# Attention followed by a SiLU layer on one core: an earlier load of the second couple's q, the first q transposed in two halves, and two re-ordered groups of instructions

## Chip, cores, metric

The kernel runs on one core of a Trainium2 chip. The metric is the device time of one execution in microseconds (us). A core has a matrix engine (TensorE, PE in the profile; PEld is its loading of weights), VectorE (DVE), ScalarE (ACT), GpSimd (POOL) and SyncE (SP), which here only issues DMAs. Each engine works off its own queue in order and waits for the others through semaphores.

## What is computed

```python
# q, k, v: (8 batches, 12 heads, 448 rows, 64), g_q, g_k: (64,)
q_n = q / sqrt(mean(q * q, -1) + 1e-6) * g_q         # k_n likewise, with g_k
scores = q_n @ k_n.T / sqrt(64)                      # per batch and head
attn = exp(scores - max) / (sum(exp(scores - max)) + 1e-9)
x = (attn @ v), heads side by side                   # (3584, 768)
h = x @ w_in                                         # w_in: (768, 2048)
out = (h * sigmoid(h)) @ w_out                       # w_out: (2048, 768)
```

## The kernel before

The heads are taken in pairs, and two pairs (four heads of one batch) are a *couple*: 24 couples, three per batch; `c` is a couple's number. One group of six couples (`GROUP` = 6) is two batches. While a group goes through attention, the first product (with `w_in`) of the group before it is computed beside it; its matrix products use seven half-size products in place of eight (class `Seven`), and so need sums and differences on VectorE and GpSimd. After all attention the rest of the first product and the whole second one follow. The gains are folded into k's transposes, and the softmax needs no maximum when the gains are small enough: a branch (line 369) tests that once, and the branch taken here is `bounded`.

**Before the branch** (lines 296 to 359) a fixed order is written out: loads of the first q, k and v on SyncE's queue, the two gains on ScalarE's, a few matmuls on the identity that only keep TensorE busy (`keep_busy`, line 342), and the root mean squares of q and k of couple 0. `Norm` does these: squares on ScalarE and their sums on VectorE (`squares`, lines 395 and 396), scaling by 1/64 on VectorE (line 420), the power -1/2 on GpSimd (line 424), the product with the rows (`scale`, line 439; on VectorE for couple 0, on GpSimd for later ones). Each of q's steps is done in two halves, one for each pair of heads.

**After it**, SyncE issues the loads of q of couples 1 and 2 and of weights; k and q of couple 0 are transposed on TensorE (lines 561 and 546) and copied out of PSUM by ScalarE (lines 563 and 547). Then `visit(c)` and `between(c)` alternate. A visit computes scores (line 579, into tiles `sc` of two banks, two of them in turn), their exponentials on ScalarE (line 584), and the products with v (`weigh`, line 611, into the banks `av0` and `av1`); the last two products of a couple are made in the next visit. Spread over the visits lie the four pieces of `normalise` for the next couple (`beside`): squares of the two halves of q, then of the two halves of k. From couple 1 to 5 the second of them stands, in the order of instructions, after the copies of the previous couple's products (line 1250), after its division (line 669) and after the reciprocals of the sums of exponentials (line 654), which are then spread over the partitions by six small DMAs (lines 660 and 662). A q piece ends, for couples below six, with the load of q two couples further on into the same buffer.

`between(c)` transposes the next couple's q and k, sums the exponentials (line 645, in a bank `mm`) and deals out two portions of other work with `fill`: matmuls of the first product are drawn one at a time from a generator until a number of columns is reached, and other instructions are dealt among them: the rounding of weights on ScalarE, VectorE and GpSimd (lines 90, 91, 113 to 120, 124), reciprocals, sums. In couples 3 to 5 the generator is `make_ahead`: for each of two blocks it makes two products of three matmuls (`two`, with `product`, line 745), the first copied out by ScalarE (line 752), the second added to it by VectorE (lines 753 and 704), and saves the result. `product` hands control back after every matmul, the last one included, so that what `fill` deals at that point comes ahead of the copy or the addition.

The order of instructions is the order of these calls; the scheduler is off (`manual_schedule`).

Of the kernel before, what the change touches and what calls it, by code (L numbers as in the profile page):

```python
# [27 lines left out]
BANK = 512  # L28
# [152 lines left out]
def kernel(  # L181
# [47 lines left out]
        left = rows[:, z.KEYS * P : z.S].rearrange("(i h) p d -> i p h d", i=2)  # L229
        return main, left  # L230

    def load_q(c, t, by_head):


        b, cp = divmod(c, z.NPAIR // 2)
        rows = q[b, ts(cp, 4)]
        if by_head:
            dst = t[0:R].rearrange("p (n j d) -> p n (j d)", n=4, j=J)
            nc.sync.dma_start(dst, rows.rearrange("n (p j) d -> p n (j d)", j=J))
            return  # L240
        for i in range(2):
            dst = t[0:R, ts(i, nq // 2)].rearrange("p (j h d) -> p j h d", j=J, h=2)
            nc.sync.dma_start(dst, rows[ts(i, 2)].rearrange("h (p j) d -> p j h d", j=J))
# [29 lines left out]
    def load_pair(state, n):  # L273
# [3 lines left out]
        for i, (name, source, bufs) in enumerate((("q", q, 2), ("k", k, 3), ("v", v, 2))):  # L277
# [15 lines left out]
    most = const.tile([1, 1], F32, name="most")  # L293
    norm = Norm(nc, z, rms, minus_half)

    first_q = room.rest[:, ds(7 * nq, nq)]
    first_squares = [spare[:, 0 : 2 * J * D], room.rest[:, ds(6 * nq, nq // 2)]]
    g1, both = (
        room.rest[0:1, ds(room.rest.shape[1] - (i + 1) * 2 * D, 2 * D)].rearrange(
            "p (two d) -> p two d", two=2  # L300
        )
        for i in range(2)
# [1 line left out]
    with tc.manual_schedule(), tc.tile_pool(  # L304
        name="ps_first", bufs=1, space=bass.MemoryType.PSUM
    ) as ps_first:
        load_q(0, first_q, True)
        load_k(0)
        for i, g in enumerate((g_q, g_k)):
            nc.scalar.dma_start(g1[:, i, :], g.rearrange("(one d) -> one d", one=1))  # L310
        load_k(1)
        load_v(0)
        load_v_rest(0)
        room.w_in.load()
        load_v_rest(1)
        nc.gpsimd.memset(minus_half, -0.5)
        make_identity(nc, ident)
        nc.scalar.activation(first, minus_half, AF.Square)


        nc.gpsimd.memset(ones[:, 0], 1.0)
        for i in range(2):
            for half in range(2):
                rows = ds(half * z.LEFT, z.LEFT)
                nc.gpsimd.memset(ones[rows, 1 + i], 1.0 if i == half else 0.0)

        wide = [g1[:, i : i + 1, :].to_broadcast([1, 2, D]) for i in range(2)]
        nc.vector.tensor_tensor(out=both, in0=wide[0], in1=wide[1], op=ALU.mult)
        nc.vector.tensor_reduce(
            out=most, in_=both[:, 0, :], axis=AX.X, op=ALU.max, apply_absolute_value=True  # L330
        )
        nc.vector.tensor_scalar(
            out=small, in0=most, scalar1=float(SCORE_MAX / D**0.5), scalar2=None, op0=ALU.is_le
        )


        idle = ps_first.tile([P, P], F32, name="idle")
        column = ps_first.tile([P, BANK], F32, name="column")[:, 0:1]

        def keep_busy(n):  # L340
            for _ in range(n):
                nc.tensor.matmul(idle, ident, ident, start=True, stop=True)

        keep_busy(4)
        nc.tensor.transpose(column, both.rearrange("p two d -> p (two d)"), ident[0:1, 0:1])
        nc.vector.tensor_scalar_mul(out=gains, in0=column, scalar1=float(D) ** -0.5)
        keep_busy(8)

        for i in range(2):
            norm.squares_q(0, first_q, first_squares[i], i)  # L350
            norm.root(0, "q", i)
        for i in range(2):
            norm.squares_k(0, place["k0"], first_squares[i], i)
            norm.root(0, "k", i)
            norm.scale(0, first_q, place["q0"], i, nc.vector)

    def arm():

        r = copy.copy(room)
        r.w_in = copy.copy(room.w_in)  # L360
        state = [dict() for _ in pairs]
        return dict(
            tc=tc, nc=nc, z=z, pairs=pairs, room=r, ring=ring, w_out=w_out, ident=ident,
            minus_half=minus_half, gains=gains, out=out,
            own=dict(NC=NC, loads=loads, place=place, norm=norm, spare=spare, ones=ones, first=first),
            plain=(state, lambda n: load_pair(state, n)),
        )

# [88 lines left out]
def bounded(  # L457
# [51 lines left out]
    for i, words in enumerate(late):  # L509
# [3 lines left out]
        low = words.rearrange("p (n two) -> p n two", two=2)[:, :, 0]  # L513
        pieces[m] = pieces[m][:2] + ((None, words), low)

    def q_of(c):
        return rows_q[c % 2 if c < GROUP else 0]

    def load_q(c):

        if 0 < c < GROUP:
            loads["q"](c, raw_q[c % 2], True)
        elif GROUP <= c < NC:
            loads["q"](c, q_of(c), False)

# [14 lines left out]
    def transpose_q(c):  # L540

        t = ps.tile([P, 2, BANK], F32, name="sc", bufs=2)
        for i in range(2):
            for j in range(J):
                rows = q_of(c)[0:R, ts(i * J + j, 2 * D)]
                nc.tensor.transpose(t[:, i, ts(j, R)], rows, ident[0:R, 0:R])  # L546
        nc.scalar.copy(qT, t[:, :, 0:S])
        if c == GROUP - 2:
            load_q(GROUP)
        elif c >= GROUP:  # L550
            load_q(c + 1)
# [121 lines left out]
    def normalise(c):  # L673


        if c >= NC:
            return []

        def piece(name, i):
            t = scratch[i if c < GROUP + 2 else 0]  # L680
            source = raw_q[c % 2] if c < GROUP else q_of(c)
            if name == "q":
                norm.squares_q(c, source, t, i)
            else:
                norm.squares_k(c, place[f"k{c % 2}"], t, i)
            if name == "q" and c < GROUP:
                norm.root(c, name, i)
                norm.scale(c, source, q_of(c), i, nc.gpsimd)
                if i == 1 and c + 2 < GROUP:
                    load_q(c + 2)  # L690
            elif i == 1:
                norm.root(c, name)
                if name == "q":
                    for m in range(2):
                        norm.scale(c, source, q_of(c), m, nc.gpsimd)

        return [lambda a=a: piece(*a) for a in (("q", 0), ("q", 1), ("k", 0), ("k", 1))]
# [34 lines left out]
    class Seven:  # L732

        def __init__(self, left, right, steps, n, done):
            self.left, self.right, self.steps, self.n, self.done = left, right, list(steps), n, done
            self.u2, self.u3 = (parts[:, ds(i * S, n)] for i in range(2))

            self.p1, self.p5 = done[1, 2], done[2, 1]  # L740

        def product(self, name):
            t, ends = bank(self.n), (self.steps[0], self.steps[-1])
            for s in self.steps:
                nc.tensor.matmul(  # L745
                    t, self.left(name, s), self.right(name, s), start=s == ends[0], stop=s == ends[1]
                )
                yield self.n
            return t

        def two(self):
            nc.scalar.copy(self.p1, (yield from self.product("1")))
            plus((yield from self.product("2")), self.p1, self.done[1, 1])

        def five(self):
            p1, u2, u3, p5, done = self.p1, self.u2, self.u3, self.p5, self.done
# [22 lines left out]
    def make_ahead(group):  # L779
        for m in range(AHEAD):  # L780
            row = staged()
            yield from part_in(group, m, [row, row]).two()
            nc.sync.dma_start(ahead[m], row)

    def fetch_ahead(group, m):
# [25 lines left out]
    def sum_x(group, c):  # L811
        right_sums(*quarters(group, c), *sums_of_x(c))

    def part_in(group, m, rows):

        chunk = 2 * m // room.CHUNK
        assert room.w_in.rounded >= (chunk + 1) * z.NW
# [19 lines left out]
            return lefts[name](c)  # L837

        done = {(i + 1, j + 1): rows[i][:, ts(j, S)] for i in range(2) for j in range(2)}
        return Seven(left, right, range(HW), S, done)  # L840

    def halves_in(group, blocks, beside=lambda m: iter(()), begun={}, fetched=()):

# [389 lines left out]
    def visit(c):  # L1233
# [7 lines left out]
            weigh(c - 1, LEFT - 1, 0)  # L1241
        if c < NC:
            scores(c, 0, 1)
        if not 0 < c < GROUP:
            run_all(beside[1:2])
        if c > 0:
            weigh(c - 1, LEFT - 1, 1)
            if c - 1 < EARLY:
                for i in range(2):
                    nc.vector.tensor_copy(x_of(c - 1, i), sums[i])  # L1250
                if inverting:
                    if c > 1:
                        divide(c - 2, None)
                    run_all(inverting)
                    inverting.clear()
            else:
                divide(c - 1, sums)
                if c < NC and c % GROUP == 0:
                    for i in range(0 if c == GROUP else 1, HW):
                        sum_x(last_two(c), i)  # L1260
                weights_in_visit(c)
            if c < GROUP:
                run_all(beside[1:2])
            if c + 1 < NC:
                loads["vrest"](c + 1)
        if c == NC:
# [18 lines left out]
    def run_all(work):  # L1285
        for piece in work:
            piece()
# [44 lines left out]
                pass  # L1332

    begun, inverting = {}, []
    for c in (1, 2):
        load_q(c)
    for _ in range(2):
        room.w_in.load()
    transpose_k(0)
# [230 lines left out]
```

## Time and profile before

| what | value |
|---|---|
| median of 3 runs | 1363.62 us (1363.23 to 1364.3) |
| the profiled execution's own time | 1364.13 us |
| its span, first to last instruction | 1362.3 us |
| granted TensorE clock, mean | 0.995 |
| PE busy | 1325.9 us, 97% |
| DVE / ACT / POOL busy | 918.5 / 517.6 / 342.7 us |
| first scores (line 579) begin | 12.35 us |
| q of couple 1 transposed (line 546), first matmul | 28.86 us |
| q of couples 2, 3, 4, 5, 6, first matmul | 46.33, 63.09, 80.59, 100.79, 125.77 us |
| PE busy from 200 to 800 us | 591.8 of 600 us |
| loads of a whole q, 448 KB, issue to landing | 4.1 us median |
| loads of k's main part, 192 KB | 3.0 us median |

In a line of the timeline the first number is the start in us, the second the duration; then come the engine, the source line, the operation, what it writes and reads with shapes, and how many instructions are merged. In brackets stands how long the engine had been idle before, and whose work ended that. One fp32 matmul appears as two records. In a table of stretches each engine's busy time is followed by its number of instructions; after the five engines come the clock granted to TensorE (1.00 is full), the busy share of the DMA engines, and GB/s.

### The profile page before, as it was taken

The numbers are of one execution on the slowest core, as the hardware profiler recorded it, in microseconds if no ns is written. First come the engines' busy times: TensorE is split into PE (matmuls) and PEld (weight loads), VectorE is DVE, ScalarE is ACT, GpSimd is POOL, SyncE is SP. The second block draws the span as 40 slices with busy tenths as digits, with TensorE's granted clock in tenths as the row PEclk, the third lists the DMA queues.
The fourth block names the chain that finished last, engine by engine and source line by source line (L and its number), as shares of the span: only waits on it lengthen the run. The fifth ranks groups of instructions, "written<-read, shape, count | busy, mean of one in ns | idle before, by whom it ended". The sixth has DMA issues, their size and how long they took to land.

```text
span 1362.3 us, 19801 instructions
## 1 busy us (share of the span) xinstructions
PE 1325.9 (97%) x7353; PEld 838.3 (62%) x7353; DVE 918.5 (67%) x1592; ACT 517.6 (38%) x884; POOL 342.7 (25%) x241
## 2 busy tenths in 40 slices
PE   7998999999999999999999999999999999999997
PEld 3333444444444444444444455556999999999997
DVE  3887867785643544644543677679878787878785
ACT  5875565565455544555554244420000000000000
POOL 4664434342332233323320134420000000000001
PEclk8999999999999999999999999999999999999999
DMA  6664445333222322322221248531413232323321
GB/s 175 183 162 108 109 135 153 92 92 90 78 76 79 93 78 78 106 78 73 71 85 44 99 134 259 175 108 43 128 61 110 74 97 74 103 82 95 108 63 38
DMA packets 175405, 139.41 MB, mean 102 GB/s; under 512 B 104036, under 2 KB 159268, under 8 KB 175300
## 3 DMA queue, kind: packets, MB, share of 16 engines
q1 hardware_dynamic: 174624, 137.08, 34.3%
q8 instruction: 60, 0.98, 0.3%
q0 software_dynamic: 352, 0.79, 0.2%
q14 instruction: 45, 0.37, 0.1%
q10 hardware_dynamic: 324, 0.20, 0.1%
HBM read 88.47 MB, written 41.29 MB: 95 GB/s over the span
## 4 chain that ended last, share of the span: by engine, by line
PE 89%; DVE 5%; issue 3%; ACT 2%; SPq 1%; DMA 0%; POOL 0%; ACTq 0%; DVEq 0%; POOLq 0%
PE mm L745 29%; PE alone L1047 22%; PE av L611 8%; PE sc L579 8%; PE mm L1047 7%; PE alone L745 7%; PE alone L1084 2%; PE sc L546 1%; PE sc L561 1%; PE sc L645 1%; PE mm L645 1%; PE mm L1084 1%; DVE work L654 1%; ACT work L584 1%; DVE work L625 1%
## 5 line engine op out<-in xcount | busy, mean ns | idle before, releaser
L745 PE MATMUL mm<-x,W 128*128 128x448 f32 x636 | 255.5, 546 | 5.2 <-DVE stage L704 2.8
L584 ACT ACTIVATE work<-sc,rms 128x448 f32<-128x448 f32 x324 | 184.3, 632 | 88.5 <-PE sc L579 76.6
L424 POOL TENSOR_TENSOR rms<-rms,minus_half 128x14 f32<-128x14 f32 (+4 forms) x55 | 138.6, 2521 | 252.3 <-DVE rms L420 200.9
L745 PEld LDWEIGHTS mm<-x,W 128*128 128x128 f32 x636 | 118.3, 191 | 127.8 <-issue 107.3
L745 PE MATMUL mm<-sums_x,W 128*128 128x448 f32 x456 | 183.0, 542 | 0.8 <-DVE parts L704 0.8
L579 PE MATMUL sc<-work 64*64 64x448 f32 x1344 | 164.9, 548 | 6.7 <-ACT work L584 4.8
L625 DVE TENSOR_TENSOR work<-work 128x896 f32<-128x896 f32 (+1 forms) x114 | 125.0, 1130 | 59.0 <-ACT work L584 57.6
L611 PE MATMUL av<-work,rows 64*64 64x448 f32 x1296 | 153.9, 549 | 7.7 <-issue 2.4
L745 PEld LDWEIGHTS mm<-sums_x,W 128*128 128x128 f32 x456 | 85.3, 190 | 86.5 <-issue 81.1
L451 POOL DMA_DIRECT2D out_dram<-x x4 | 2.2, 565 | 442.7 <-DVE x L704 442.7
L611 PEld LDWEIGHTS av<-work,rows 64*64 64x64 f32 x1296 | 51.9, 133 | 96.4 <-issue 86.3
L579 PEld LDWEIGHTS sc<-work 64*64 64x64 f32 x1344 | 52.0, 134 | 89.6 <-issue 35.3
L396 DVE TENSOR_REDUCE rms<-squares 112x8 f32<-112x512 f32 (+1 forms) x80 | 52.4, 656 | 73.8 <-ACT squares L395 73.0
L1047 PE MATMUL alone<-W,rows 128*128 128x192 f32 x488 | 92.0, 326 | 0.0
L760 POOL TENSOR_TENSOR parts<-parts,stage 128x448 f32<-128x448 f32 x31 | 42.0, 1356 | 163.7 <-DVE parts L704 163.5
L1047 PEld LDWEIGHTS alone<-W,rows 128*128 128x128 f32 x488 | 81.4, 190 | 0.0
L1047 PE MATMUL alone<-W,work 128*128 128x192 f32 x382 | 72.2, 326 | 0.0
L878 ACT ACTIVATE stage<-stage 128x896 f32<-128x896 f32 x63 | 57.3, 945 | 26.1 <-DVE stage L704 25.4
L1047 PEld LDWEIGHTS alone<-W,work 128*128 128x128 f32 x382 | 63.8, 190 | 0.0
L654 DVE RECIPROCAL work<-sc 128x224 f32<-128x224 f32 x36 | 55.7, 1548 | 11.1 <-PE sc L645 11.1
L1057 ACT COPY squares<-alone 128x192 f32<-128x192 f32 x34 | 10.8, 318 | 136.9 <-PE alone L1047 78.4
L395 ACT ACTIVATE squares<-rows 128x512 f32<-128x512 f32 (+1 forms) x74 | 44.7, 605 | 47.1 <-DVE rms L396 46.3
(242 smaller groups left out, 2117.4 us busy)
## 6 DMA issues: line engine op xcount, KB each, us to landing
hidden<-stage SPq DMA_DIRECT2D x63, 448.0 KB, 2.8
work<-hidden SPq DMA_DIRECT2D x21, 1024.0 KB, 5.5
rows<-in_moe_w_out_dram SPq DMA_DIRECT2D x32, 384.0 KB, 3.2
W<-in_moe_w_in_dram SPq DMA_DIRECT2D x22, 512.0 KB, 5.1
rows<-in_k_dram SPq DMA_DIRECT2D x48, 192.0 KB, 3.0
work<-work SPq DMA_DIRECT2D x144, 56.0 KB, 1.9
rows<-in_q_dram SPq DMA_DIRECT2D x36, 224.0 KB, 3.5
x<-hidden SPq DMA_DIRECT2D x7, 1024.0 KB, 5.9
```

The lines of the kernel that those rows point to most:

```text
L395: nc.scalar.activation(t, rows, AF.Square)
L396: nc.vector.tensor_reduce(out=out, in_=t.rearrange("p (n d) -> p n d", n=n), axis=AX.X, op=ALU.add)
L424: nc.gpsimd.tensor_tensor(out=t, in0=t, in1=half, op=ALU.pow)
L579: nc.tensor.matmul(two[ds(half * D, D), h, 0:S], keys[rows, ts(half, D)], qT[rows, pair, :], start=True, stop=True,)
L584: nc.scalar.activation(eleft[:, h] if j == LEFT else weights(c, j)[:, i, h], two[:, h, 0:S], AF.Exp, scale=norm.column(c, i, h, j),)
L611: nc.tensor.matmul(sums[i][ds(h * D, D), :], v, w, start=(j == 0 and step == 1), stop=(j == LEFT - 1 and step == 1),)
L625: nc.vector.tensor_tensor(out=total, in0=total, in1=more, op=ALU.add)
L654: nc.vector.reciprocal(out=r[0][:, rows], in_=t[:, rows])
L745: nc.tensor.matmul(t, self.left(name, s), self.right(name, s), start=s == ends[0], stop=s == ends[1])
L760: nc.gpsimd.tensor_tensor(out=u2, in0=u2, in1=p5, op=ALU.add)
L878: nc.scalar.activation(t, t, AF.Silu)
L1047: nc.tensor.matmul(t, x[:, i], y, start=i == ORDER[0], stop=i == ORDER[-1])
```

## The change

- The first q is loaded in two halves, one per pair of heads.
- The load of q of couple 1 goes ahead of the branch, behind the first k, into a place of its own (`second_q`, the last 1024 columns of `room.rest`); the gains' scratch moves to make room. The load of v of couple 0 follows it, ahead of k of couple 1. After the branch only q of couple 2 is loaded. As couple 1's q has its own place, the load of couple 3's q no longer waits for couple 1's scaling.
- Of the twelve `keep_busy` matmuls the last four are left out.
- Couple 0's q: the transposes of the first pair go to a bank of `sc`, those of the second to `av1`; ScalarE copies the first (448 columns), VectorE the second.
- In visits 1 to 5 the second q piece (sum over the second half's squares, power, scaling, load of a later q) goes directly behind the copies of line 1250, ahead of division and reciprocals; in visit 6 it goes behind the division.
- In `make_ahead` control is handed back after the copy or addition, not between it and the last matmul.

In the compiled order TensorE differs only in the four matmuls left out and in the bank; VectorE has one copy more; on ScalarE and VectorE the copies and additions of `two` stand before the rounding that they followed; on SyncE the load of a later q stands ahead of the six spread DMAs of the same visit in visits 1 and 2 (visit 3 has none).

```diff
-    def load_q(c, t, by_head):
+    def load_q(c, t, by_head, steps=1):
...
         if by_head:
-            dst = t[0:R].rearrange("p (n j d) -> p n (j d)", n=4, j=J)
-            nc.sync.dma_start(dst, rows.rearrange("n (p j) d -> p n (j d)", j=J))
+            for i in range(steps):
+                n = 4 // steps
+                dst = t[0:R, ts(i, nq // steps)].rearrange("p (n j d) -> p n (j d)", n=n, j=J)
+                nc.sync.dma_start(dst, rows[ts(i, n)].rearrange("n (p j) d -> p n (j d)", j=J))
             return
...
-    first_q = room.rest[:, ds(7 * nq, nq)]
+    first_q, second_q = (room.rest[:, ds(i * nq, nq)] for i in (7, 8))
...
-        load_q(0, first_q, True)
+        load_q(0, first_q, True, 2)
         load_k(0)
+        load_q(1, second_q, True)
+        load_v(0)
         for i, g in enumerate((g_q, g_k)):
             nc.scalar.dma_start(g1[:, i, :], g.rearrange("(one d) -> one d", one=1))
         load_k(1)
-        load_v(0)
         load_v_rest(0)
...
-        keep_busy(8)
+        keep_busy(4)
...
+    def raw_of(c):
+        return own["second_q"] if c == 1 else raw_q[c % 2]
...
     def transpose_q(c):
         t = ps.tile([P, 2, BANK], F32, name="sc", bufs=2)
+        both = [t[:, i] for i in range(2)]
+        if c == 0:
+            both[1] = ps.tile([P, BANK], F32, name="av1")
         for i in range(2):
             for j in range(J):
                 rows = q_of(c)[0:R, ts(i * J + j, 2 * D)]
-                nc.tensor.transpose(t[:, i, ts(j, R)], rows, ident[0:R, 0:R])
-        nc.scalar.copy(qT, t[:, :, 0:S])
+                nc.tensor.transpose(both[i][:, ts(j, R)], rows, ident[0:R, 0:R])
+            if c == 0:
+                (nc.scalar.copy, nc.vector.tensor_copy)[i](qT[:, i], both[i][:, 0:S])
+        if c > 0:
+            nc.scalar.copy(qT, t[:, :, 0:S])
...
     class Seven:
...
                 nc.tensor.matmul(
                     t, self.left(name, s), self.right(name, s), start=s == ends[0], stop=s == ends[1]
                 )
-                yield self.n
+                if not (self.prompt and s == ends[1]):
+                    yield self.n
             return t
         def two(self):
             nc.scalar.copy(self.p1, (yield from self.product("1")))
+            if self.prompt:
+                yield self.n
             plus((yield from self.product("2")), self.p1, self.done[1, 1])
+            if self.prompt:
+                yield self.n
...
     def visit(c):
...
-        if not 0 < c < GROUP:
+        if c == 0:
             run_all(beside[1:2])
         if c > 0:
             weigh(c - 1, LEFT - 1, 1)
             if c - 1 < EARLY:
                 for i in range(2):
                     nc.vector.tensor_copy(x_of(c - 1, i), sums[i])
+                run_all(beside[1:2])
                 if inverting:
...
             else:
                 divide(c - 1, sums)
+                run_all(beside[1:2])
...
-            if c < GROUP:
-                run_all(beside[1:2])
...
-    for c in (1, 2):
-        load_q(c)
+    load_q(2)
```

`make_ahead` calls `part_in(group, m, [row, row], True)`, which hands `prompt=True` to `Seven`.

More of the change, by code (lines that the diff above doesn't have):

```diff
@@ L294 @@
     norm = Norm(nc, z, rms, minus_half)
-    first_q = room.rest[:, ds(7 * nq, nq)]
+    first_q, second_q = (room.rest[:, ds(i * nq, nq)] for i in (7, 8))
     first_squares = [spare[:, 0 : 2 * J * D], room.rest[:, ds(6 * nq, nq // 2)]]
     g1, both = (
-        room.rest[0:1, ds(room.rest.shape[1] - (i + 1) * 2 * D, 2 * D)].rearrange(
+        room.rest[0:1, ds(6 * nq + nq // 2 + i * 2 * D, 2 * D)].rearrange(
             "p (two d) -> p two d", two=2
@@ L364, in arm @@
             minus_half=minus_half, gains=gains, out=out,
-            own=dict(NC=NC, loads=loads, place=place, norm=norm, spare=spare, ones=ones, first=first),
+            own=dict(
+                NC=NC, loads=loads, place=place, norm=norm, spare=spare, ones=ones, first=first,
+                second_q=second_q,
+            ),
             plain=(state, lambda n: load_pair(state, n)),
@@ L521, in load_q @@
         if 0 < c < GROUP:
-            loads["q"](c, raw_q[c % 2], True)
+            loads["q"](c, raw_of(c), True)
         elif GROUP <= c < NC:
@@ L680, in piece @@
             t = scratch[i if c < GROUP + 2 else 0]
-            source = raw_q[c % 2] if c < GROUP else q_of(c)
+            source = raw_of(c) if c < GROUP else q_of(c)
             if name == "q":
@@ L732, in bounded, with __init__ @@
     class Seven:
-        def __init__(self, left, right, steps, n, done):
+        def __init__(self, left, right, steps, n, done, prompt=False):
             self.left, self.right, self.steps, self.n, self.done = left, right, list(steps), n, done
+            self.prompt = prompt
             self.u2, self.u3 = (parts[:, ds(i * S, n)] for i in range(2))
@@ L781, in make_ahead @@
             row = staged()
-            yield from part_in(group, m, [row, row]).two()
+            yield from part_in(group, m, [row, row], True).two()
             nc.sync.dma_start(ahead[m], row)
@@ L812, in sum_x, with part_in @@
         right_sums(*quarters(group, c), *sums_of_x(c))
-    def part_in(group, m, rows):
+    def part_in(group, m, rows, prompt=False):
         chunk = 2 * m // room.CHUNK
@@ L839, in part_in @@
         done = {(i + 1, j + 1): rows[i][:, ts(j, S)] for i in range(2) for j in range(2)}
-        return Seven(left, right, range(HW), S, done)
+        return Seven(left, right, range(HW), S, done, prompt)
     def halves_in(group, blocks, beside=lambda m: iter(()), begun={}, fetched=()):
```

## The prediction

> **What bounds the kernel.** I read the page first, then busy time in stretches cut at the transposes of each couple's q (line 546), then TensorE's timeline for the first 165 us, and for each gap the timeline of the engine named in the brackets.
>
> ```profile
> PE 1325.9 (97%) x7353; PEld 838.3 (62%) x7353; DVE 918.5 (67%) x1592; ACT 517.6 (38%) x884; POOL 342.7 (25%) x241
> ```
>
> TensorE (PE) is busy 97% of 1362.3 us; what is left is mostly at the start. Stretches (us; then busy time and instructions of PE, PEld, DVE, ACT, POOL; granted clock; DMA share; GB/s):
>
> ```profile
> 0.00:12.35 12.35, 7.44 (x41) 6.72 (x41) 5.12 (x14) 5.70 (x8) 6.86 (x16) 1.00 0.78 187
> 12.35:28.86 16.51, 12.33 (x89) 3.60 (x89) 4.54 (x9) 8.81 (x16) 8.02 (x6) 0.79 0.68 191
> 28.86:46.33 17.47, 16.48 (x155) 6.64 (x151) 12.91 (x20) 14.90 (x26) 7.74 (x7) 1.00 0.56 173
> 100.79:125.77 24.98, 21.78 (x165) 8.59 (x162) 17.42 (x24) 14.30 (x25) 10.57 (x6) 0.93 0.37 99
> ```
>
> Couple 0 (second row) loses most: PE idles 4.2 of 16.5 us, and its clock is reduced. From 200 us on PE is 98.5% busy or more until the last stretch, and every stage follows the one before in the same queues, so a microsecond won early should stay won. The gaps, by PE's timeline (start, duration, what; idle before it and its releaser):
>
> ```profile
> 12.35 1.73 PE L579 MATMUL sc<-work 64*64 64x448 f32 x16 [1.00 <-ACT work L547]
> 18.85 1.77 PE L579 MATMUL sc<-work 64*64 64x448 f32 x8 [3.20 <-ACT work L584]
> 47.32 0.60 PE L546 MATMUL sc<-ident,rows 112*128 112x112 f32 x4 [0.39 <-POOL rows L439]
> 64.75 0.60 PE L546 MATMUL sc<-ident,x 112*128 112x112 f32 x4 [1.05 <-POOL x L439]
> 82.22 0.60 PE L546 MATMUL sc<-ident,rows 112*128 112x112 f32 x4 [1.03 <-POOL rows L439]
> 110.66 3.36 PE L745 MATMUL mm<-x,W 128*128 128x448 f32 x4 [2.76 <-DVE stage L704]
> 132.41 2.52 PE L745 MATMUL mm<-x,W 128*128 128x448 f32 x6 [0.99 <-ACT stage L752]
> 141.74 1.12 PE L611 MATMUL av<-work,rows 64*64 64x448 f32 x6 [1.02 <-DVE x L669]
> ```
>
> The 3.20 us name ScalarE (ACT), but ACT itself waited: the squares of q of couple 1 stand ahead of the exponentials in its queue, and their load was issued only at 12.95, behind the branch.
>
> ```profile
> 17.12 0.63 ACT L395 ACTIVATE squares<-x 112x512 f32<-112x512 f32 x1 [2.50 <-DMA x<-in_q_dram]
> 17.65 1.14 ACT L584 ACTIVATE work<-sc,rms 128x448 f32<-128x448 f32 x2
> ```
>
> VectorE (DVE) explains the next ones: two reciprocals (2.96 us) stand ahead of the sums of q's second half, and 1.5 us of weight rounding ahead of the addition that frees a bank.
>
> ```profile
> 40.41 2.96 DVE L654 RECIPROCAL work<-mm 128x224 f32<-128x224 f32 x2
> 43.28 0.62 DVE L396 TENSOR_REDUCE rms<-x 112x8 f32<-112x512 f32 x1
> ...
> 108.52 0.36 DVE L113 TENSOR_SCALAR W<-W 128x512 f32<-128x512 f32 x1
> 108.92 0.43 DVE L116 TENSOR_SCALAR W<-W 128x512 int32<-128x512 int32 x1
> 109.38 0.69 DVE L120 SCALAR_TENSOR_TENSOR W<-W 128x512 int32<-128x512 int32 x1
> 109.99 0.62 DVE L704 TENSOR_TENSOR stage<-mm,stage 128x448 f32<-128x448 f32 x1
> ```
>
> [...] eight matmul records of line 579 take 0.98 us at 14.67 and 1.77 after the 3.2 us gap; the clock by the microsecond is 0.50 from 18.3 to 25.1 and again from 110.7 to 114.0. At the start the clock column reads 1.00, but the warming matmuls of line 342 last 421 ns each until 8.0 us and about 300 after; there I trust the durations. [...] Here the pair of line 625 takes 2.10 us at 27.45 and 2.94 at 45.28, beside POOL's scaling at 45.91.
>
> **Start.** Loading q in two halves wins nothing by itself: the first sum (line 396, 5.64) stands in DVE's queue behind the gains (line 346, until 5.60), which wait for g_k at 4.81. So POOL's powers and both scalings (8.39, 10.00) stay, and the second pair's transposes run at 10.75 to 11.35. Then PE waited for one ACT copy of both halves (0.91 us) until 12.35. Now ACT copies half 0 while PE waits for half 1, and DVE copies half 1 (as line 1250: 0.61); the first scores need only half 0 and start at 11.35: 1.0 won. DVE's copy comes behind its own branch (SP's takes 1.2 us, 11.74 to 12.95), hence at about 11.9 to 12.5; it delays only the second scores, needed by ACT at 14.0. The four warming matmuls left out (1.7 us at low clock) are covered by k's seven transposes, which move up to about 7.1, if k has landed. SP issues one DMA more ahead of k (0.4 us), and k then lands by about 7.5 (3.35 + 0.4 + 3.7 us, median of line 250). That is a bare cover: see rival one.
>
> **Couple 0.** With q of couple 1 issued at some 4.5 us instead of 12.95, ACT never waits for it. Its queue is then 14 exponentials of 0.52 (two occupy 1.04: 37.61 to 38.64), three squares of 0.52 and one of 0.42: 9.3 us without a break. The first exponentials start at 12.46 (scores 11.35 + 0.98 + 0.13). Walked through: pairs at 12.5, 14.0, 15.6, 16.6, 18.2, 19.7; PE follows with scores at 18.6 and the last two products of line 611 (0.75 each) at 19.7 and 20.5, the last scores at 21.25, and couple 1's transposes at 22.1 instead of 28.86. That is 6.7, with the 1.0 of the start in it, at full clock. [...] I take 6.5, both ends 5.4 and 7.0. What is late next is ACT. The other loads keep up: about 5.4 MB before 23 us, at the 265 GB/s that 10 to 20 us shows, is 20 us, and what comes last (weights, k of couple 2) is used after 26.
>
> **Couples 1 to 3.** The sum over q's second half goes ahead of reciprocals and division. POOL's second power and scaling (1.63 + 1.04) then follow its first without waiting, and the second transposes find their rows. The three stalls are 0.39, 1.05, 1.03. Not all is won: the same DVE work now precedes k's sums and line 625, so the last exponentials come up to 0.3 later; against it, scaling falls on reciprocals, not on line 625, which may save up to 0.8 there. The reciprocals end up to 0.8 later, and so does their spread by six DMAs: in couple 3 DVE waited 0.49 for it already (division, 86.02), and couple 4's weighing waits for DVE's copies behind that. In visits 1 and 2 the load of q for couple c+3 now stands ahead of the spread in SP's queue and waits for POOL's scaling: some 0.6 us for the spread and the loads of v and k behind, which have 1.8 us to spare or more (rivals). I take 0.4 (0 to 0.5), 0.7 (0 to 1.05), 0.4 (-0.3 to 1.0).
>
> **Products made ahead.** The addition of line 704 moves ahead of lines 113 to 120: 0.36 + 0.43 + 0.69 of 1.5 us gone, with 1.3 us of PE's stall left (the reciprocal at 107.05 is still ahead). I take 1.4 (1.0 to 1.5). A gap of 1.3 us should not lower the clock: the stretch after couple 0's first scores was only some 55% busy and stayed at full clock. Four records took 3.36 us instead of 1.68: 1.5 more (0 to 1.65). The copy of line 752 for the second product comes as soon as PE ends at 131.42, not at 131.85: 0.4 (0 to 0.5); behind it wait a rounding and k's squares on ACT, covered by the 2.52 us until the exponentials at 136.0. The first such copy moves ahead of exponentials at 89.79 and ends before them: nothing.
>
> **Couple 6.** Division goes ahead of the sum of q's second half, which had waited 0.85 for ACT; PE's 1.02 shrinks to nothing, but DVE is nearly full until 165: 0.7 (0 to 1.0).
>
> **Sum.** 6.5 + 0.4 + 0.7 + 0.4 + 1.4 + 1.5 + 0.4 + 0.7 = 12.0. The profiled execution took 1364.13 (span 1362.3 and 1.8 around it): 1352.1, its span 1350.3. The median of the runs, 1363.62, lies 0.5 lower: 1351.6. The low ends sum to 6.1, the high ends to 14.2: 1357.5 and 1349.4.
>
> **Rivals.** *The clock stays low.* With half of the warming gone and k late, [...] PE paces it: eleven groups of 1.49 from 11.35 end at 27.8, so 1.1 is won instead of 6.5; with the clock lost at 110 us too, 5.1 is left: 1358.5. For it: the bare cover. Against: dense work warmed in 3.3 us at 110.7, in 6.3 at 18.85. *Other engines take the place.* DVE is busy 9.6 of 10 us at 40 and 9.4 at 80; if its queue sets the pace, all after couple 0 is lost: 1357.1. *SP's queue, the slower end.* In visits 1 and 2 the q load holds up v for the next couple. Issued at 69.33 with 3.3 us to land, v(3) has 1.8 us to spare before its weighing at 74.45; v(2) 3.2. From there on every microsecond that POOL's scaling ends after the reciprocals is lost; at 10 us late both visits lose 15 together, against 12.0 won: 1366.6. POOL's two powers and two scalings are 6 us from the first sum, though, and end about with the reciprocals.
>
> **Chances.** Forecast 0.67; clock 0.10; other engines 0.12; more than counted (about 1348) 0.03; gains mostly absorbed, within 0.2%, 0.04; SP's queue 0.04. A measurement tells about 0.2% (2.7 us) from no change: faster 0.92, same 0.04, slower 0.04. The range 1349.4 to 1357.5 holds the forecast, most of the second rival and the better part of the first one's cases: 0.8.
>
> **What would show it.** No wait of line 395 for the q load; first scores near 11.4; couple 1's transposes near 22; clock at 1.00 from 12 to 30 us; no POOL waits at line 546; the gap of line 745 near 100 us (107.9 less what is won before) 1.3 long with a full clock behind it. A clock of 0.5 after 12 us, or DVE waits in front of line 611 in couple 4, would make it wrong.

## The result and the profile after

| | before | changed |
|---|---|---|
| median of 4 runs each | 1363.42 us (1362.93 to 1364.3) | 1353.18 us (1352.74 to 1354.56) |
| ratio, 95% interval | | 0.9926 [0.9909, 0.9943] |
| profiled execution, its span | 1364.13, 1362.3 us | 1352.74, 1350.9 us |
| granted clock, mean | 0.995 | 0.998 |

The change wins 10.2 us by the medians and 11.4 us between the two profiled executions (that of before lies 0.7 above its median, that of the changed kernel 0.4 below). The forecast was 1351.6, and a gain of 12.0 in the profile. The sum held, but three of its terms did not. The kernel before varies more than the changed one: of 21 further runs of it six took 1359.7 to 1361.0 at a mean clock of 0.998, the others 1362.1 to 1365.7, most of them at 0.994 to 0.997, so part of the 10 us is low clock that not every execution loses.

The lines of the changed kernel are 3 to 21 higher: 439 became 445, 546 became 558, 579 became 594, 584 became 599, 611 became 626, 704 became 719, 745 became 761. First the page's busy times, then the stretches that answer to those of before (between the same matmuls: first scores, q of couples 1 and 2, and the last one from q of couple 5 to q of couple 6):

```profile
PE 1321.1 (98%) x7345; PEld 836.3 (62%) x7345; DVE 916.6 (68%) x1593; ACT 516.4 (38%) x884; POOL 344.7 (26%) x241
```

```profile
0.00:10.05 10.05, 7.35 (x32) 6.04 (x33) 5.10 (x14) 5.33 (x8) 5.80 (x15) 1.00 0.78 190
10.05:20.97 10.92, 9.46 (x90) 2.96 (x89) 5.23 (x10) 8.48 (x16) 8.36 (x7) 1.00 0.84 239
20.97:38.45 17.48, 16.48 (x155) 6.64 (x151) 12.92 (x20) 14.81 (x26) 9.96 (x8) 1.00 0.81 218
92.52:114.14 21.62, 20.10 (x166) 8.13 (x162) 16.58 (x24) 13.88 (x24) 11.17 (x6) 1.00 0.45 118
```

Busy times barely moved: TensorE is busy for 4.8 us less, because eight warming records (four matmuls) are gone and less of its work ran at the low clock (0.50 from 18.5 to 25.3 and from 110.7 to 114.0 before; over the first 140 us the granted clock averages 0.96 before and 1.00 after). The time came out of waits. The start is 2.30 us shorter (12.35 to 10.05), couple 0 is 5.59 shorter (16.51 to 10.92) and now at full clock, couple 1 is not shorter at all (17.47 to 17.48), and the stretch with the first products is 3.36 shorter.

TensorE's gaps in the same order as before (start, duration, what; in brackets the idle time and what ended it):

```profile
10.05 1.84 PE L594 MATMUL sc<-work 64*64 64x448 f32 x16
20.97 0.98 PE L558 MATMUL sc<-ident,x 112*128 112x112 f32 x8
57.48 0.99 PE L576 MATMUL sc<-ident,rows 128*128 128x128 f32 x7 [1.00 <-ACT work L599]
74.72 0.98 PE L576 MATMUL sc<-ident,rows 128*128 128x128 f32 x7 [0.93 <-ACT work L599]
86.17 1.12 PE L626 MATMUL av<-work,rows 64*64 64x448 f32 x6 [0.59 <-DVE x L1271]
100.65 1.77 PE L761 MATMUL mm<-x,W 128*128 128x448 f32 x4 [1.24 <-DVE stage L719]
120.41 2.52 PE L761 MATMUL mm<-x,W 128*128 128x448 f32 x6 [0.62 <-ACT stage L769]
137.20 0.60 PE L558 MATMUL sc<-ident,rows 112*128 112x112 f32 x4 [0.68 <-POOL rows L445]
```

The three waits for POOL at q's transposes are gone, and two waits for ScalarE of nearly the same length stand a few matmuls later. The wait before the third product fell from 2.76 to 1.24, and the same four records take 1.77 instead of 3.36. Two short waits are new, at 86.17 and 137.20. The gain, read off as before less after at the same matmul. The last column but one is the same step in a second profile of the changed kernel (the control, below), and shows which steps repeat:

| up to | before | after | gain | the step's own gain | in the control | forecast |
|---|---|---|---|---|---|---|
| first scores | 12.35 | 10.05 | 2.30 | 2.30 | 2.37 | 1.0 |
| q of couple 1 | 28.86 | 20.97 | 7.89 | 5.59 | 5.59 | 5.5 |
| sums (line 645, now 660) before the first products' last gap | 103.44 | 94.95 | 8.49 | 0.60 | 0.12 | 1.5 |
| scores of couple 5, behind that gap | 113.94 | 102.35 | 11.59 | 3.10 | 3.10 | 2.9 |
| second block's product behind the copy of line 752 | 132.41 | 120.41 | 12.00 | 0.41 | 0.40 | 0.4 |
| products with v in couple 6 | 141.74 | 129.54 | 12.20 | 0.20 | 1.20 | 0.7 |
| first product behind q of couple 7 | 148.88 | 137.64 | 11.24 | -0.96 | -0.88 | 0 |
| end of the span | 1362.3 | 1350.9 | 11.4 | 0.16 | 0.4 | 0 |

### The profile page after: what moved, and what is told of

Its sections match the earlier page's. It is cut to its first block, busy times and chain, and to the rows that moved or that the text cites. A ratio compares the mean times of both kernels' runs of the same rounds, so it can differ in the third digit from the quotient of the medians.

```text
span 1350.9 us, 19783 instructions
## 1 busy us (share of the span) xinstructions
PE 1321.1 (98%) x7345; PEld 836.3 (62%) x7345; DVE 916.6 (68%) x1593; ACT 516.4 (38%) x884; POOL 344.7 (26%) x241
## 4 chain that ended last, share of the span: by engine, by line
PE 86%; DVE 6%; issue 2%; DMA 2%; ACT 2%; SPq 1%; POOL 0%; DVEq 0%; ACTq 0%; POOLq 0%
PE mm L761 27%; PE alone L1068 22%; PE av L626 8%; PE mm L1068 7%; PE alone L761 7%; PE sc L594 7%; PE alone L1105 2%; PE sc L558 1%; PE sc L576 1%; PE sc L660 1%; DVE work L669 1%; DMA work<-work 1%; PE mm L1105 1%; DMA hidden<-stage 1%; DVE work L640 1%
```

## The experiments

Each ratio is to the kernel before on the same chip. The changed kernel itself was run again beside three of them, as control: 1352.44 us (6 runs), ratio 0.9927 [0.9914, 0.9941], profiled at a span of 1350.0, 12.3 less than before. Two executions of one kernel thus differ by 0.9 in the profile, and less than about 2 us between two kernels is not settled by medians; for such steps the traces decide.

> The changed kernel itself once more, as the measure for the kernels beside it on the same chip. Theory A: 1352.5 to 1354.5 us; [...] the clock may fall for some 3 us between 10 and 14 us in this execution (two kernels with the same start showed that), which moves its first products by 0.4 to 0.6 us. Rival (no part for the clock): the same milestones as in the first profile within 0.2 us.

The clock stays full in it (1.00 in every microsecond from 4 to 18, mean 0.998 over the execution), and all steps up to 120.83 but one agree with the first profile. Where they differ, a small DMA that spreads the reciprocals landed earlier or later. TensorE at couple 4's and couple 6's products with v:

```profile
86.58 1.12 PE L626 MATMUL av<-work,rows 64*64 64x448 f32 x6 [1.05 <-DVE x L1271]
128.96 1.11 PE L626 MATMUL av<-work,rows 64*64 64x448 f32 x6
```

The wait at couple 4 is 1.05 instead of 0.59, and the one at couple 6, 0.82 in the first profile, is gone. In VectorE's queue the divisions ahead of them wait for their spread, by the trace 2.07 and 0.39 us here, and 1.61 and 1.47 there.

### The start: the first q whole again

```diff
-        load_q(0, first_q, True, 2)
+        load_q(0, first_q, True)
```

> The changed kernel, but with the first q loaded in one piece as before; nothing else differs. Theory A (the halved load ends the wait for the first half and lets the tiny gains through the DMA engines 1.1 us earlier, 3.71 against 4.81 us, and VectorE's first sums and GpSimd's powers start that much earlier): the gains land near 4.8 again, first scores near 11.2 instead of 10.05, time 1.0 to 1.2 us above the changed kernel. Rival (what was predicted: halving the load wins nothing, the earlier gains come from something else, as the order of the loads behind): first scores stay near 10.0 and the time stays.

Measured: 1354.92 us, ratio 0.9947 [0.9926, 0.9968], span 1352.8. The transposed gains appear on TensorE at 5.13 instead of 4.05, q's second transposes at 10.60 instead of 9.52, the first scores at 11.13 instead of 10.05. So 1.08 of the 2.30 comes from the halved load. Another 0.15 goes with this execution's q, which landed about that much sooner than before's (squares at 4.84 for 4.98). The cause is in VectorE's first instruction, which needs both gains; here it is before and after (timeline of VectorE):

```profile
4.81 0.28 DVE L328 TENSOR_TENSOR W<-W 1x128 f32<-1x128 f32 x1 [4.81 <-DMA W<-in_g_k_dram]
```

```profile
3.71 0.28 DVE L331 TENSOR_TENSOR W<-W 1x128 f32<-1x128 f32 x1 [3.71 <-DMA W<-in_g_k_dram]
```

The gains are 256 bytes each, issued by ScalarE at 0.73 and 1.3 in both kernels, yet they land 1.1 us sooner when SyncE's q is cut. VectorE's first instruction starts at 3.19 to 3.71 in the nine profiles with the halves, and at 4.79 to 5.10 in the three without. Within the halves the exact moment counts little: in the control it starts 0.50 earlier, and the first scores come 0.07 earlier, since VectorE then waits 0.34 for ScalarE's squares. In both kernels they land beside the first piece of q: the squares of q's first half start at 4.98 and at 3.58. How the gains are held up, the traces do not show.

### The halved load alone

```diff
-        load_q(0, first_q, True)
+        load_q(0, first_q, True, 2)
```

(in the kernel before, with the helper's new parameter).

> The kernel before with one edit: the first q is loaded in two halves. Theory A (a large load holds back the small loads of the gains, and half of it lets them land about 1.1 us earlier): the multiplication of the gains starts near 3.7 instead of 4.81, all steps of couple 0's norms start about 1.1 earlier, first scores near 11.2 instead of 12.35, whole time about 1 us less than before, near the edge of what is measurable. Rival (the prediction's step): loading q in two halves wins nothing by itself, gains at 4.8, first scores at 12.35. If the halves gain but couple 1's q then comes no earlier, its stall grows and takes it back: first scores near 11.2 and a wait of 4.2 in place of 3.2.

Measured: 1362.71 us (14 runs), ratio 1.0001 [0.9991, 1.0012]. The first scores come at 11.16, 1.19 earlier, and nothing is left of it. TensorE's second gap, then SyncE's load of couple 1's q (timelines of this experiment):

```profile
19.16 1.77 PE L581 MATMUL sc<-work 64*64 64x448 f32 x8 [4.70 <-ACT work L586]
```

```profile
13.44 0.88 SPq L241 DMA_DIRECT2D x<-in_q_dram  x2
```

The wait grew from 3.20 to 4.70. SyncE reaches that load only after the loads ahead of the branch and the branch, and these do not get shorter when the norms do: 12.95 before, 13.44 here, since one more DMA is issued. An earlier start is worth nothing while the next input is as late as before. The prediction's sentence that the halves win nothing by themselves is thus right of the whole kernel, and its reason is wrong.

### The early load alone, and everything but it

Alone, in the kernel before:

```diff
         load_k(0)
+        load_q(1, second_q, True)
...
-    for c in (1, 2):
-        load_q(c)
+    load_q(2)
```

> The kernel before, with one part of the change: q of couple 1 loaded ahead of the branch, behind the first k, into its own place. Theory A: the stall of 3.2 us before line 579 and the low clock behind it go; the start stays at 12.35 and the later waits stay; transposes of couple 1's q near 23.2 (28.86 less 5.6), time 5.3 to 5.9 us under the kernel before. Rival (the clock needs the whole change, since the second transposes wait longer): clock of 0.5 somewhere between 12 and 20 us and only 3.2 us won.

Measured: 1358.66 us (17 runs), ratio 0.9973 [0.9965, 0.998], span 1356.6. The wait of 3.20 and the low clock behind it are gone (the clock reads 1.00 in every microsecond from 5 to 20); q of couple 1 is transposed at 23.49, 5.37 earlier than before, and the lead is 5.38 at the third product (110.66 to 105.28). The first scores come 0.22 later than before, at 12.57, so the stretch of couple 0 alone takes 10.92, the same as in the changed kernel. All later waits stay: 0.39, 1.05 and 1.03 for POOL, 2.76 for the addition.

Everything but it, in the changed kernel:

```diff
-        load_q(1, second_q, True)
...
-    load_q(2)
+    for c in (1, 2):
+        load_q(c)
```

> The change without its early load: q of couple 1 is issued behind the branch as before, into its own place, all else as changed. If the parts add up (theory): the whole gain of 10 to 11 us less the 4.3 to 5.7 us that the early load gave alone leaves 5 to 6, about 1357.5 to 1358.5; the wait for the second scores returns, about 3 to 4 us long. Rival (the early load is worth more inside the change, because the earlier first scores only reach couple 1 if its q is there): the wait is longer by what the start won less what the branch comes earlier, and 3.5 to 4.5 us are left, about 1359.5.

Measured: 1360.25 us (22 runs), ratio 0.998 [0.9973, 0.9986], span 1358.1.

```profile
12.39 0.98 PE L593 MATMUL sc<-work 64*64 64x448 f32 x8 [0.48 <-ACT work L598]
19.41 1.77 PE L593 MATMUL sc<-work 64*64 64x448 f32 x8 [6.04 <-ACT work L598]
```

First scores at 10.07 and the scores behind the gap at 19.41, even 0.56 later than before: the whole 2.3 us of the start went into a wait of 6.04. Q of couple 1 follows at 29.34, 0.48 later than before. By the profiled spans the two parts alone win 5.7 and 4.2, together 9.9 of 11.4; by the medians 4.3 (1362.93 to 1358.66, on that chip) and 3.2 (1363.48 to 1360.25), 7.5 of 10.2. What is missing, 1.5 to 2.7, is about the start's 2.3 us, which count only with the early load. These sums are not far above the scatter; the two traces settle it. Additivity, the first theory, falls; the rival stands.

### Copies of q by pairs

```diff
-        if c == 0:
-            both[1] = ps.tile([P, BANK], F32, name="av1")
...
-            if c == 0:
-                (nc.scalar.copy, nc.vector.tensor_copy)[i](qT[:, i], both[i][:, 0:S])
-        if c > 0:
-            nc.scalar.copy(qT, t[:, :, 0:S])
+        nc.scalar.copy(qT, t[:, :, 0:S])
```

> The changed kernel with couple 0's q transposed and copied as before, both pairs into one tile and one ScalarE copy for both. Theory A: first scores 1.0 us later after the second transposes (the ScalarE copy of 0.91 stands between), everything behind 0.8 to 1.0 us later. Rival (covered, as the exponentials set the pace): less than 0.3 us.

Measured: 1355.22 us, ratio 0.9953 [0.9934, 0.9972], 2.8 behind the control, more than was expected. First scores at 11.29 (control 9.98, changed kernel 10.05), behind a wait of 0.99 for ScalarE's one copy. Of these 1.24 to 1.31 the copies account for 1.07: from q's second transposes to the first scores it takes 1.60 here (9.69 to 11.29) as in the kernel before, and 0.53 in the changed one. The rest is that the second transposes come some 0.2 later in this execution. Forecast was 1.0. Together with the halves' 1.08 and the 0.15 of q's landing this is the start's 2.30. From the first scores to q of couple 1 it took 11.71 instead of 10.92: its clock was low in between (0.63 over 10 to 14), which is the next point.

### The second group of warming matmuls

```diff
-        keep_busy(4)
```

(the second of the two calls).

> The changed kernel without the four warming matmuls behind the gains. Theory A [...]: clock low over couple 0's first scores, until 14 to 18 us; 0.4 to 1.5 us slower. Rival [...]: within 0.3 us.

Measured: 1354.73 us, ratio 0.994 [0.9922, 0.9958], 2.3 behind the control. Without them k's transposes wait 1.19 for k at 5.34, 24 records of the first scores take 4.09 from 10.58 (16 take 1.84 in the changed kernel), and q of couple 1 comes at 22.29 instead of 20.90. So they are worth 1.4 there; the rest of the 2.3 appears in small pieces later and was not followed.

Without these four matmuls the first rival's low clock is thus there, by these durations. With them it was met too, but as a fall from full clock. In the changed kernel and the control it stayed full (16 records of the first scores in 1.84 us). In three variants whose start is the same or nearly so (old order of q's pieces, old unloading, one copy) it fell to 0.50 between 10.3 and 11.0 and came back some 3.4 us later (3.40, 3.42 and 3.42 by stretches of 1 us). Stretches, first of the changed kernel, then of the old order of q's pieces (TensorE's busy time is the first number behind the comma; the clock is the third from the right):

```profile
7.00:10.00 3.00, 2.28 (x12) 1.56 (x11) 2.17 (x5) 1.96 (x3) 3.00 (x3) 1.00 1.18 274
10.00:14.00 4.00, 2.93 (x30) 0.69 (x29) 1.48 (x3) 2.84 (x6) 1.71 (x3) 1.00 0.81 161
```

```profile
7.00:10.00 3.00, 1.71 (x15) 1.11 (x19) 2.19 (x6) 1.97 (x3) 3.00 (x2) 1.00 1.16 256
10.00:14.00 4.00, 4.00 (x24) 0.82 (x20) 1.48 (x3) 2.62 (x6) 1.41 (x2) 0.57 0.87 172
```

Over all executions in which q's second transposes, just before the first scores, ran at full speed (four records in 0.60 us; 1.01 without these four matmuls), TensorE was busy 1.46, 1.71 and 1.72 us from 7 to 10 where the clock fell, and 1.86 (the kernel below, with k behind the addition), 2.01, 2.03, 2.28 and more where it did not. The longest gap in these 3 us, where the clock fell, is 0.94, 0.72 and 0.86. It is a pattern over one execution each; what makes the clock fall was not tested, and the 3 us are the author's choice. From 6 to 9 us the two groups separate as well, from 8 to 10 they do not (0.91 to 1.28 against 1.16 and more). Part of the higher busy time is itself slowness: q's first four transposes take 0.89 at 7.91 in the changed kernel and 0.60 at 7.99 in the old-order one, which was at full speed sooner. The two were not told apart. From the first scores to q of couple 1 the old-order variant takes 11.34 instead of 10.92, the one-copy variant 11.71: the fall costs 0.4 to 0.8, since ScalarE sets the pace of most of couple 0 (in the changed kernel it is busy without a break from 12.21 to 19.64).

### The order of q's pieces

The old place in the changed kernel:

```diff
-                run_all(beside[1:2])
                 if inverting:
...
+            if c < GROUP:
+                run_all(beside[1:2])
```

> The changed kernel, with the second q piece of visits 1 to 6 back where it stood before (behind division and reciprocals, in visit 6 ahead of the division). Rival (the prediction's sum: 0.4 + 0.7 + 0.4 + 0.7): 2.2 us slower than the changed kernel. Theory A (read from the trace after: 0.6 won for couple 2, 0.2 for couple 3, 0.2 for couple 4, 0.7 lost again at couple 4's weighing, and at couples 6 and 7 0.2 won and 1.0 lost): the re-ordering is worth nothing or a small loss; this kernel takes the same time as the changed one or up to 0.7 us less, with the waits on GpSimd at line 558 back (0.4 to 1.1 each) and no wait at couple 4's weighing.

Measured: 1352.54 us, ratio 0.9929 [0.9908, 0.995], span 1350.9, the same as with the change. The waits of 0.39, 1.05 and 1.03 for POOL are back (at 39.65, 57.08 and 74.55), and those of 1.00, 0.93 and 0.59 are gone. So the re-ordering is worth nothing that can be measured. What took its place in couple 2 is in VectorE's queue of the changed kernel:

```profile
50.99 2.96 DVE L669 RECIPROCAL work<-mm 128x224 f32<-128x224 f32 x2
53.87 0.62 DVE L402 TENSOR_REDUCE rms<-squares 128x8 f32<-128x512 f32 x1
54.42 0.53 DVE L402 TENSOR_REDUCE rms<-x 128x6 f32<-128x384 f32 x1
54.98 0.17 DVE L426 TENSOR_SCALAR rms<-rms 128x14 f32<-128x14 f32 x1
55.07 2.10 DVE L640 TENSOR_TENSOR work<-work 128x896 f32<-128x896 f32 x2
```

ScalarE's last exponentials of the couple wait for line 640, by the trace 2.94 us, until 56.27, and TensorE waits for them. With the old order the same pair takes 2.93, as it did before, beside POOL's scaling at 55.66:

```profile
55.04 2.93 DVE L640 TENSOR_TENSOR work<-work 128x896 f32<-128x896 f32 x2
```

ScalarE's exponentials start at 56.24, nearly the same time. So the two orders are two ways into one bound: VectorE's queue from the copies to line 640.

Next, k's second sum behind line 640 (and visit 6 in its old order):

```diff
         scores(c, 2, 0)
-        if c < GROUP:
-            run_all(beside[3:4])
         weigh(c, 1, 1)
...
         run_all(add(c, 1))
+        if c < GROUP:
+            run_all(beside[3:4])
```

> The changed kernel with two re-orderings: in visit 6 q's second piece again ahead of the division, and in visits 0 to 5 the second piece of k (sums of squares, power) behind the addition of line 640, so that the last exponentials no longer wait behind it. Theory A (the waits moved to the addition behind VectorE's reciprocals): the 1.0 and 0.9 us that line 576 waits for the exponentials shrink to 0.2 to 0.4, and the 0.7 us wait on GpSimd near 137 us goes; 1.0 to 2.0 us faster than the changed kernel. Rival (VectorE's whole queue sets the pace there, in whatever order): within 0.4 us of the changed kernel.

Measured: 1352.14 us, ratio 0.9924 [0.991, 0.9938], span 1349.2; beside the control 0.3 and 0.8 better, less than the 1.0 to 2.0 that were expected and not enough to call. TensorE's gaps in this kernel:

```profile
56.69 0.98 PE L576 MATMUL sc<-ident,rows 128*128 128x128 f32 x7 [0.37 <-ACT work L599]
65.66 0.98 PE L626 MATMUL av<-x,rows 64*64 64x448 f32 x8 [0.50 <-DVE rms L402]
73.51 0.98 PE L576 MATMUL sc<-ident,rows 128*128 128x128 f32 x7 [0.18 <-ACT work L599]
85.62 1.12 PE L626 MATMUL av<-work,rows 64*64 64x448 f32 x6 [1.25 <-DVE x L1271]
129.21 1.12 PE L626 MATMUL av<-work,rows 64*64 64x448 f32 x6 [1.02 <-DVE x L684]
```

Waits of 1.00 and 0.93 shrink to 0.37 and 0.18, as that reading of VectorE's queue demands; 0.66 of it comes back at 85.62 (1.25 for 0.59; the control has 1.05 there). Visit 6's old order takes away the 0.68 at 137 and brings the 1.02 back at 129.21.

### The old unloading of the first products

```diff
-part_in(group, m, [row, row], True).two()
+part_in(group, m, [row, row]).two()
```

> The changed kernel, with the copies and additions of the products made ahead back behind what is dealt out there. Theory A: the stall before line 761 is 2.7 to 2.8 us again and the clock falls to 0.5 for 3.3 us behind it, the second product's copy is 0.4 later: 3.5 to 3.9 us slower than the changed kernel, of which 1.6 by the clock. Rival (the clock stays up[...]): 1.9 to 2.2 us slower.

Measured: 1355.8 us, ratio 0.9951 [0.9933, 0.9969], span 1354.0: 3.1 more than the changed kernel by the spans, 2.6 by the medians (3.4 more than the control).

```profile
103.00 3.25 PE L761 MATMUL mm<-x,W 128*128 128x448 f32 x4 [2.76 <-DVE stage L719]
```

The gap of 2.76 and the slow four records are back, with the clock at 0.50 from 103 to 106; the gap at 124.62 is 1.00 again instead of 0.62. From the matmul ahead of the first gap (99.22 here) to 124.62 it takes 25.40 us, in the changed kernel (98.39 to 120.41) and in the control 22.02: 3.4 for the two steps, where 2.9 and 0.4 were forecast. By couple 7's q (139.95) it is 3.41 behind the control and only 2.75 behind the first profile, which alone of the three has the wait of 0.82 in couple 6.

## Why the prediction was right, and where it was not

**Start: wrong in size, 1.0 against 2.30.** The step that failed is "Loading q in two halves wins nothing by itself: the first sum ... stands in DVE's queue behind the gains ..., which wait for g_k at 4.81. So POOL's powers and both scalings ... stay". The queue was read rightly; that g_k's landing would stay at 4.81 was assumed. Undoing the halves costs 1.08, so this is shown. The copies by pairs gave 1.07 for 1.0: that term was right.

**Couple 0: right, 5.59 for 5.5.** With the early load alone it was 5.59 too. ScalarE is full from 12.21 to 19.64, as was worked out. (The low clock of the kernel before, given as 18.3 to 25.1, reads 18.5 to 25.3 in finer stretches.) What the prediction did not say is that this load also decides whether the start counts: without it 2.3 us of start turn into a wait.

**Couples 1 to 3: wrong, 0.60 for 1.5, and 0.12 in the control.** The transposes of couple 2's q gave 0.6, those of couples 3 and 4 0.2 each; 0.7 of that went at couple 4's products with v (86.17), 0.2 came back behind them. The step that failed is "the last exponentials come up to 0.3 later; against it ... may save up to 0.8": the exponentials were already about to bind. In the old order they end 0.3 before the second transposes do (56.24 + 1.16 against 57.08 + 0.60), so hardly more than that was to be won where 1.05 was in sight. The second rival, VectorE's queue, had the right engine, for these couples alone. The spread behind the later reciprocals, named in the prediction, grew from a wait of 0.49 to 1.61 of VectorE's division (2.07 in the control); the trace gives the wait, and no run separated it. The SP rival cost nothing that can be seen, but the slack of 1.8 us that was counted for v of couple 3 is used up: from its issue to its first matmul it is 5.12 us before (69.33 to 74.45) and 3.31 after (62.45 to 65.76), where 3.3 was counted for the landing, and the run with the old unloading shows a first, short wait for it:

```profile
66.76 0.98 PE L626 MATMUL av<-x,rows 64*64 64x448 f32 x8 [0.19 <-DMA rows<-in_v_dram]
```

**Products made ahead and the clock: right, 3.10 for 2.9**, and the gap left, 1.24, was 1.3 in the forecast; **copy: right, 0.41 for 0.4.**

**Couple 6: wrong, -0.76 for 0.7, and 0.32 in the control.** The step that failed is "PE's 1.02 shrinks to nothing, but DVE is nearly full until 165: 0.7": it gave POOL's scaling, which the re-ordering delays, no price. The wait did go in the control; in the first profile, where the division waited 1.47 for its spread, 0.82 was left. Both lost about 0.9 right behind it: the sum over q's second half now stands behind the division, and POOL's second scaling became late for couple 7 (0.68). The old order of visit 6 exchanges one wait for the other, which shows this second half. Why the spread landed 1.1 us later in one execution than in the other, no run shows.

The terms were thus 1.3 too low at the start and 2.4 too high in the re-ordered pieces (1.4 and 1.8 in the control); the sum, 12.0 for 11.4 in the profile and 12.3 in the control, owes part of its accuracy to these two cancelling, which is luck.

## What to carry to other kernels

Follow the instruction that a queue waits for back to its own cause: here two loads of 256 bytes landed 1.1 us sooner once a load of 448 KB on another queue was cut in two. A start that is made shorter counts only if the next input comes as early; try both edits together and each alone. Before an instruction is moved ahead in a full queue, list what then stands behind it and how near each of these is to binding: here three waits of 2.5 us were removed and nearly all came back under another engine's name.

## What was not expected of the hardware

- Two loads of 256 bytes, issued at the same time as before, landed at 3.19 to 3.71 instead of 4.79 to 5.10 when a load of 448 KB on another queue was split into two (nine profiles and three).
- The granted clock fell to 0.50 for some 3.4 us (3.40 to 3.42), from 10.3 to 11.0 on, in executions in which TensorE had been busy 1.46 to 1.72 of the 3 us before, in short pieces with no gap over 1 us, and not where it had been busy 1.86 or more. One execution each: a pattern, whose cause was not tested.
